# Another planned order for a two-part kernel, with five stores of 20 columns and three stores cut by rows

## The chip, the core and the metric

The kernel runs on one core of one Trainium2 chip. A core has a matrix engine (TensorE, PE in the profile), three other compute engines (VectorE = DVE, ScalarE = ACT, GpSimd = POOL) and SyncE (SP), each with its own in-order instruction stream, and sixteen DMA engines that move data between memory (HBM) and the core's on-chip memory. The metric is the device time of one execution in microseconds (us); the times given are medians of several runs.

## What is computed

```python
B, N, C = (4, 6400, 256)                       # q, k, v, float32
qn = q / (norm(q, axis=1) + 1e-06)             # the norm of each column over the 6400 rows
kn = k / (norm(k, axis=1) + 1e-06)
s = kn.transpose(0, 2, 1) @ qn / tau           # 256 x 256 for each of the 4 batches
a = softmax(s)
x = (v @ a).reshape(25600, 256)
# a mixture of 8 adapters of rank 16 on every row of x, the two best by x @ w_gate, softmax over the two
logits = x @ w_gate
for e in the two best:  x_out += w[e] * ((x @ A[e]) @ B[e])
```

All of q, k and v must have been read before the last row is written: 78.9 MB are read from HBM and 26.2 MB are written.

## The kernel before, in words

A batch has 6400 rows; partition p of the 128 holds rows 50p to 50p+49, called columns here, so a column is 128 rows of 256 numbers, 1 KB for each partition in float32. q and k are loaded in three pieces of 17, 17 and 16 columns (the names q10, q11, q12 stand for batch 1; a word such as q10 in the order loads the pair from q and k), v in five pieces of ten columns (v10 to v14). GpSimd issues all these loads (L578); they become bf16 on the way. Named steps, with the lines that issue them:

- G (L587 to L605): for each column, TensorE adds k'q to the accumulator (L593) and the squares that the norms need (L597 for k, L602 for q). For the groups of columns in OFF, the squares are left out here; ScalarE squares the group instead (sq, L615), VectorE adds the groups up (add, L621; red, L627) and TensorE sums over partitions at the end (n2p).
- After a batch's last column: norms, softmax and the product of a with the gate and A weights (n2, rsqrt, rq_ps, exp, aT, waA; L648 to L765), one short chain through three engines.
- For each piece of v: T transposes it (L788) and Te copies it out of PSUM; then either ZL (L812, gate logits and adapter inputs in one product, for the pieces in MERGED) or log (L826) and later Z (L879); a row of ten small gate steps on VectorE with one tanh on ScalarE; Ze (L890), gzT (L902), and Y (L915, L920), whose result Ye copies to the output tile y (L769 on ScalarE, L771 on VectorE).
- store (L928): SyncE issues the write of a piece of y, ten columns, 1280 KB. The last two pieces of the last batch go in parts of 4, 4 and 2 columns.

The order of all this comes from a planner in the file (Plan.run, L95): a list scheduler with a duration for each step and each engine, a rank from the place in WORDS (L402), and numbered buffers (STORE, L220: six banks of PSUM, six q/k tiles, three v tiles, four vT, seven y). It emits the steps in the order in which it started them, and each engine then executes its own in that order. HOLD (L409) names stores that must wait for a load: a tiny DMA that reads the last elements of the loaded tile (do_hold, L640, on SP ahead of the store) makes SP wait for the load's landing. OUT (L77) lets eight loads be on the way. SP's DMAs and ACT's use eight semaphores in turn; a DMA whose semaphore was last used by the DMA eight places before waits until that one has landed.

Of the kernel before, what the change touches and what calls it, by code (L numbers as in the profile page):

```python
# [18 lines left out]
class Step:  # L19
# [3 lines left out]
    def __init__(self, key, eng, deps, rank, take, give, size=0.0):  # L23
        self.packet = max(size, 0.08)
        self.key, self.eng, self.deps, self.rank = key, eng, deps, rank
        self.take, self.give, self.size = take, give, size
        self.users, self.place = [], {}
        self.ready, self.end, self.on = 0.0, None, None
        self.left = len(deps)
        self.only = next(iter(eng)) if len(eng) == 1 else None  # L30


class Clock:


    WINDOW, FIRST, LOW, HIGH = 3.413, 0.31, 0.5, 0.8
# [29 lines left out]
    SPARE = 1.0  # L66


class Plan:

    LAT = 0.07
    DMA_LAT = 1.8
    ENGINES = ("PE", "DVE", "ACT", "POOL", "SP")
    ISSUE = 0.55
    ISSUE_LAT = 1.8
    STORE_LAT = 1.4
    OUT = 8  # L77

# [15 lines left out]

    def run(self, head):  # L95
# [4 lines left out]
        loads, queue, stores = list(self.loads), [], []  # L100
        now, out, left = 0.0, 0, sum(s.key[0] != "warm" for s in self.steps.values())
        free["POOL"] = 0.2
        clock = Clock()

# [5 lines left out]
        def can_take(s):  # L110
            return all((kind, name) in held or self.store[kind] for kind, name in s.take)

        def start(s, eng):
            for kind, name in s.take:
                if (kind, name) not in held:
                    held[kind, name] = self.store[kind].pop(0)
                    s.place[kind] = held[kind, name]
            s.on = eng
            s.t = now
            self.out.append(s)  # L120

# [5 lines left out]
        while left:  # L127
            again = False
            if (loads and free["POOL"] <= now + 1e-9 and out < self.OUT and can_take(loads[0])):
                s = loads.pop(0)  # L130
                start(s, "POOL")
                out += 1
                free["POOL"] = now + self.ISSUE
                push(free["POOL"], "free", None)
                push(now + self.ISSUE_LAT, "asked", s)
                again = True
            for e in self.ENGINES:
# [3 lines left out]
                for s in wait[e]:  # L141
                    if not can_take(s) or (s.key[0] == "warm" and not clock.idle(now)):
                        continue
# [3 lines left out]
                    if best is None or (s.rank, s.seq) < (best.rank, best.seq):  # L147
                        best = s
# [9 lines left out]
                else:  # L158
                    push(free[e], "end", best)
# [3 lines left out]
            busy = [x for x in (queue, stores) if x]  # L163
            t = events[0][0] if events else float("inf")
            base = max(now, head)

            share = sum(x[0].packet for x in busy)
            if busy:
                t = min(t, base + min(x[0].size / x[0].packet for x in busy) * share)
            assert t < float("inf"), [s.key for s in self.steps.values() if s.end is None][:20]  # L170
            if t > base:
                for x in busy:
                    x[0].size -= (t - base) * x[0].packet / share
                    if x[0].size < 1e-6:
                        push(t + self.DMA_LAT, "landed", x[0])
                        out -= x is queue
                        x.pop(0)
            now = max(now, t)
            while events and events[0][0] <= now + 1e-9:
                _, _, what, s = heapq.heappop(events)  # L180
                if what == "asked":
                    queue.append(s)
                elif what == "store":
                    stores.append(s)
# [3 lines left out]
                elif what == "landed":  # L188
                    push(now + (SAFE if s.on == "POOL" else 0.0), "end", s)
                    for u in s.users:  # L190
                        if u.key[0] == "hold":
                            u.left -= 1
                            if u.left == 0:
                                push(now, "ready", u)
                elif what == "end":
# [6 lines left out]
                    for u in s.users:  # L202
                        u.left -= u.key[0] != "hold"
                        if u.left == 0 and u.eng and u.key[0] != "hold":
                            push(now + (0.0 if s.on == u.only else self.LAT), "ready", u)
# [5 lines left out]
NC = 50  # L211
# [4 lines left out]
V = ((0, 1), (1, 1), (2, 1), (3, 1), (4, 1))  # L216
# [13 lines left out]

def make_plan(B, order, ahead):
# [6 lines left out]
    for kind, b, i in order:  # L238
        if kind == "v":
            p.add(("load", "v", b, i, V[i][0] * PC, V[i][1] * PC), {}, (), 0, take=(("v", (b, i)),),  # L240
                  size=LOAD * V[i][1] * PC + 0.062)
            continue
        for c, n in PARTS.get((b, i), QK[i:i + 1]):
            for h in "qk":
                p.add(("load", h, b, i, c, n), {}, (), 0, take=(("qk", (h, b, i)),), size=LOAD * n + 0.062)

    for h in "qk":
        p.add(("cast", h), {"ACT": 0.6}, [("load", h, 0, 0) + PARTS[0, 0][0]], 0)
    p.loads[2].size += 0.5
    for b in range(B):  # L250

        for i, (c0, n) in enumerate(QK):
            for c in range(c0, c0 + n):
# [8 lines left out]
                p.add(("G", b, c), {"PE": 0.442 - 0.112 * sum((b, group_of(c), w) in OFF for w in "kq")}, deps,  # L262
# [4 lines left out]
        for w in "kq":  # L267
# [5 lines left out]
            for x, g in enumerate(halves):  # L273
                c, n = GROUPS[g]
                i = max(i for i, q in enumerate(QK) if q[0] <= c)
                p.add(("sq", w, b, g), {"ACT": 0.2 + 0.2125 * n},
                      [k for k in p.steps if k[:4] == ("load", w, b, i) and k[4] < c + n and c < k[4] + k[5]]
                      + [("cast", w)] * ((b, c) == (0, 0)), pos["qk", b, i] - SQ, take=(("ssq", (w, b)) if x == 0 else ("sq", (w, b, g)),),
                      give=(("qk", (w, b, i)),))
                if x:  # L280
                    p.add(("add", w, b, g), {"DVE": 0.15 + 0.268 * n},
# [4 lines left out]
            if halves:  # L286
                p.add(("red", w, b), {"DVE": 1.9}, [before], pos["qk", b, len(QK) - 1] - 1, give=(("ssq", (w, b)),))
                p.add(("n2p", w, b), {"PE": 0.35}, [("red", w, b), ("G", b, NC - 3)], -100, take=(("bank", ("n2p", w, b)),))
                late.append(w)
        if b == 0:  # L290
            p.add(("wts",), {"DVE": 1.8}, [("load", "k", 0, len(QK) - 1) + PARTS[0, len(QK) - 1][1]], -200)
# [3 lines left out]
        p.add(("accs", b, 1), {"ACT": 0.38}, [end], ch)  # L295
        p.add(("n2", b, 0), {"DVE": 0.45}, [end], ch)
        p.add(("accs", b, 0), {"ACT": 0.38}, [("n2", b, 0)], ch)
        p.add(("n2", b, 1), {"DVE": 0.45}, [("accs", b, 1)], ch)
        p.add(("rsqrt", b), {"DVE": 1.9 + 0.2 * len(late)},
              [("n2", b, 0), ("n2", b, 1)] + [("n2p", w, b) for w in late], ch, take=(("port", b),),  # L300
              give=(("port", b),) + tuple(("bank", ("n2p", w, b)) for w in late))
        p.add(("rq_ps", b), {"PE": 0.45}, [("rsqrt", b)], ch, take=(("bank", ("rq", b)),))
        for ic in range(2):
            p.add(("s", b, ic), {"DVE": 0.42}, [("rq_ps", b), ("accs", b, ic)], ch, give=(("bank", ("rq", b)),))
            p.add(("exp", b, ic), {"ACT": 0.68}, [("s", b, ic)], ch)
            p.add(("aT_ps", b, ic), {"PE": 0.14}, [("exp", b, ic)], ch, take=(("bank", ("aT", b)),))
        p.add(("recip", b), {"DVE": 0.17}, [("exp", b, 0), ("exp", b, 1)], ch)
        p.add(("aT", b), {"DVE": 0.42}, [("aT_ps", b, 0), ("aT_ps", b, 1)], ch, give=(("bank", ("aT", b)),))
        p.add(("waA_ps", b), {"PE": 0.35}, [("aT", b), ("wts",)], ch, take=(("bank", ("waA", b)),))
        p.add(("waA", b, 0), {"DVE": 0.35}, [("waA_ps", b), ("recip", b)], ch, give=(("bank", ("waA", b)),))  # L310
        p.add(("waA", b, 1), {"ACT": 0.38}, [("waA_ps", b), ("recip", b)], ch, give=(("bank", ("waA", b)),))
        p.add(("a", b), {"DVE": 0.5}, [("recip", b), ("aT", b)] + [("a", b - 1)] * (b > 0), ch + 1)

        for i in range(NP):
            v = max(g for g, (i0, _) in enumerate(V) if i0 <= i)
            x = pos["v", b, v] + 0.3 * (i - V[v][0])
            for u, (c, n) in enumerate(UNITS):
                p.add(("T", b, i, u), {"PE": 0.112 * n + 0.01}, [("load", "v", b, v, V[v][0] * PC, V[v][1] * PC)], x - ahead,
                      take=(("vT", (b, i)), ("bank", ("T", b, i, u))),
                      give=(("v", (b, v)),) if u == len(UNITS) - 1 else ())  # L320
                p.add(("Te", b, i, u), {"DVE": 0.16 + 0.125 * n, "ACT": 0.17 + 0.213 * n},
                      [("T", b, i, u)], x - ahead, give=(("bank", ("T", b, i, u)),))
            merged = (b, i) in MERGED
            if merged:
                for z, (c, n) in enumerate(ZUNITS):
                    p.add(("ZL", b, i, z), {"PE": 0.1145 * n + 0.005},
                          [("Te", b, i, u) for u, (c0, n0) in enumerate(UNITS) if c0 < c + n and c < c0 + n0]
                          + [("waA", b, ic) for ic in range(2)], x - ahead,
                          take=(("bank", ("ZL", b, i, z)), ("zl", (b, i))))
                    p.add(("ZLe", b, i, z), {"ACT": 0.17 + 0.1145 * n, "DVE": 0.14 + 0.142 * n},  # L330
                          [("ZL", b, i, z)], x - ahead, give=(("bank", ("ZL", b, i, z)),))
                prev = [("ZLe", b, i, z) for z in range(len(ZUNITS))]
            else:
                p.add(("log", b, i), {"PE": 0.55},
                      [("Te", b, i, u) for u in range(len(UNITS))] + [("waA", b, ic) for ic in range(2)], x - ahead,
                      take=(("bank", ("log", b, i)), ("gate", (b, i))))
                p.add(("loge", b, i), {"ACT": 0.27, "DVE": 0.27}, [("log", b, i)], x - ahead,
                      give=(("bank", ("log", b, i)),))
                prev = [("loge", b, i)]
            for name, eng, t in (("m1", "DVE", .27), ("eq1", "DVE", .27), ("lm", "DVE", .27),  # L340
                                 ("m2", "DVE", .27), ("msum", "DVE", .19), ("t", "DVE", .27),
# [645 lines left out]
```

## Time and profile before

| | |
|---|---|
| Median of 3 runs | 254.41 us (254.39 to 254.47) |
| The profiled execution | 254.46 us, its span (first to last instruction) 252.7 us: 1.8 us lie around it |
| Busy: PE, DVE, ACT, POOL | 217.8, 192.7, 151.1, 27.1 us |
| TensorE's granted clock | 0.986 of full |
| DMA packets | 11243, 66.70 MB |
| DMA queues, share of sixteen engines' span | loads 74.4%, stores and the first small loads 26.1%, ACT's first loads 0.8%, instructions 0.4% and 0.1% |
| Warm-up matmuls (L777), which only keep PE busy | 39 |

How to read it: the busy time of an engine says how much it did; what sets the end is told by the waits and by the chain that ended last. A DMA engine's share over 1.00 means that its packets overlap a little. For each DMA the trace also holds sixteen landing events, one for each DMA engine; they carry a time but not the engine's number, so the first and the last of the sixteen tell how far the engines are apart.

### The profile page before, as it was taken

The page shows a single profiled execution, that of the slowest core. Times are in us where ns is not written, and L with a number is a line of the kernel's source. Part 1 is how long each engine was busy: PE and PEld are TensorE (multiplying, and loading weights), DVE is VectorE, ACT ScalarE, POOL GpSimd, SP SyncE. Part 2 cuts the span into 40 slices and gives each one's busy share as a digit, 9 for nine tenths or more (in the row PEclk, how much of TensorE's full clock was granted, in tenths as well). Part 3 has the DMA queues.
Part 4 walks back from the last instruction along what each step waited for, and adds up shares of the span by engine and source line. Part 5 has one row for each costly group of instructions (what it writes and reads, how often), then busy time and mean ns, then how long its engine had stood idle before and what let it go on. Part 6 is the DMA issues. An engine that isn't in the chain of part 4 may idle for free.

```text
span 252.7 us, 5852 instructions
## 1 busy us (share of the span) xinstructions
PE 217.8 (86%) x2357; PEld 193.0 (76%) x2357; DVE 192.7 (76%) x528; ACT 151.1 (60%) x269; POOL 27.1 (11%) x54
## 2 busy tenths in 40 slices
PE   0274995988999998689999999889999979999990
PEld 0162882876999996579899899779999769999980
DVE  0055589869899987588899899489898898889850
ACT  5454427546786543975667768362674846657671
POOL 7003010040002002000500100500000000000000
PEclk9998899999999999999999999999999999999997
DMA  8999999999999999999999999999999999999996
GB/s 251 217 217 209 211 223 208 217 218 215 215 217 241 303 305 298 224 213 221 210 215 220 215 217 217 211 212 313 317 251 353 322 341 317 337 392 415 404 408 249
DMA packets 11243, 66.70 MB, mean 264 GB/s; under 512 B 1360, under 2 KB 1744, under 8 KB 6608
## 3 DMA queue, kind: packets, MB, share of 16 engines
q0 software_dynamic: 6912, 38.80, 74.4%
q1 hardware_dynamic: 3968, 26.87, 26.1%
q10 hardware_dynamic: 336, 0.66, 0.8%
q8 instruction: 18, 0.29, 0.4%
q14 instruction: 9, 0.07, 0.1%
HBM read 78.91 MB, written 26.21 MB: 416 GB/s over the span
## 4 chain that ended last, share of the span: by engine, by line
PE 53%; DMA 32%; issue 5%; DVE 4%; ACT 2%; POOL 1%; POOLq 0%; DVEq 0%
DMA v<-in_v_dram 18%; PE Y_ps L915 13%; PE acc L593 10%; DMA qk<-in_q_dram 10%; PE Y_ps L920 6%; PE T_ps L788 5%; PE ZL_ps L812 5%; DMA qk<-in_k_dram 5%; PE gzT_ps L902 4%; PE acc L597 3%; PE acc L602 2%; PE Z_ps L879 1%; ACT a_exp L715 1%; DVE a_bf L763 1%; PE log_ps L826 1%
## 5 line engine op out<-in xcount | busy, mean ns | idle before, releaser
L593 PE MATMUL acc<-qk 128*128 128x256 bf16 x400 | 69.6, 282 | 17.0 <-DMA qk<-in_k_dram 9.4
L915 PE MATMUL Y_ps<-a_bf,vT 128*128 128x256 bf16 x400 | 60.0, 273 | 0.2 <-DVE acc_sb L710 0.2
L621 DVE TENSOR_TENSOR ssq<-ssq,sq 128x1280 f32<-128x1280 f32 (+1 forms) x27 | 43.4, 1606 | 19.6 <-ACT sq L615 19.6
L769 ACT COPY y<-Y_ps 128x512 f32<-128x512 f32 x79 | 46.2, 586 | 16.6 <-PE Y_ps L920 13.5
L593 PEld LDWEIGHTS <-qk 128*128 128x128 bf16 x400 | 34.2, 101 | 20.7 <-DMA qk<-in_k_dram 11.5
L615 ACT ACTIVATE sq<-qk 128x1280 f32<-128x1280 bf16 (+1 forms) x27 | 36.9, 1368 | 17.7 <-DVE ssq L621 16.6
L915 PEld LDWEIGHTS <-vT 128*128 128x128 bf16 x400 | 38.9, 98 | 4.7 <-issue 0.3
L920 PE MATMUL Y_ps<-ball,gzT 128*128 128x256 bf16 x200 | 38.2, 273 | 0.0
L597 PE MATMUL acc<-qk 128*128 128x128 bf16 x242 | 34.5, 224 | 0.0
L788 PE MATMUL T_ps<-ident,v 128*128 128x128 f32 x200 | 27.6, 274 | 0.6 <-DVE waA_sb L757 0.4
L769 ACT COPY vT<-T_ps 128x512 f32<-128x512 f32 (+1 forms) x44 | 21.2, 510 | 10.9 <-PE T_ps L788 10.5
L597 PEld LDWEIGHTS <-qk 128*128 128x128 bf16 x242 | 24.4, 101 | 3.5
L890 DVE TENSOR_TENSOR gz<-zl,gateg 128x256 bf16<-128x256 f32 x70 | 26.3, 445 | 0.3
L578 POOL DMA_DIRECT2D v<-in_v_dram x20 | 11.5, 576 | 133.7 <-PE T_ps L788 92.8
L788 PEld LDWEIGHTS T_ps<-ident,v 128*128 128x128 f32 x200 | 22.3, 141 | 1.6 <-DVE waA_sb L757 0.6
L602 PE MATMUL acc<-qk 128*128 128x128 bf16 x168 | 23.4, 222 | 0.0
L902 PE MATMUL gzT_ps<-ident,gz 128*128 128x128 f32 x100 | 20.9, 281 | 2.6 <-DVE gateg L868 1.4
L920 PEld LDWEIGHTS <-gzT 128*128 128x128 bf16 x200 | 19.6, 98 | 2.3
L812 PE MATMUL ZL_ps<-waA_sb,vT 128*128 128x136 bf16 x280 | 19.5, 223 | 1.7 <-DVE waA_sb L757 1.5
L771 DVE COPY gzT<-gzT_ps 128x256 f32<-128x256 f32 (+1 forms) x40 | 15.0, 380 | 7.1 <-PE gzT_ps L902 5.6
L812 PEld LDWEIGHTS <-vT 128*128 128x128 bf16 x280 | 17.7, 98 | 2.4 <-issue 2.1
L615 ACT ACTIVATE ssq<-qk 128x1536 f32<-128x1536 bf16 x8 | 11.9, 1489 | 11.4 <-DMA qk<-in_q_dram 7.4
(80 smaller groups left out, 271.3 us busy)
## 6 DMA issues: line engine op xcount, KB each, us to landing
out_dram<-y SPq DMA_DIRECT2D x18, 1280.0 KB, 16.7
v<-in_v_dram POOLq DMA_DIRECT2D x20, 640.0 KB, 20.5
qk<-in_q_dram POOLq DMA_DIRECT2D x7, 1088.0 KB, 23.7
qk<-in_k_dram POOLq DMA_DIRECT2D x7, 1088.0 KB, 28.4
qk<-in_q_dram POOLq DMA_DIRECT2D x4, 512.0 KB, 19.2
qk<-in_k_dram POOLq DMA_DIRECT2D x4, 512.0 KB, 22.5
qk<-in_q_dram POOLq DMA_DIRECT2D x2, 1024.0 KB, 19.4
qk<-in_k_dram POOLq DMA_DIRECT2D x2, 1024.0 KB, 23.8
```

Source lines behind the costliest of these rows:

```text
L593: nc.tensor.matmul(acc[ic][:, 0:256], kt[:, j, ic::CC], qt[:, j, :], start=c == 0, stop=False, skip_group_check=True)
L597: nc.tensor.matmul(acc[ic][:, 256:384], kt[:, j, ic::CC], kt[:, j, ic::CC], start=False, stop=False, skip_group_check=True)
L602: nc.tensor.matmul(acc[ic][:, 384:512], qt[:, j, ic * P:(ic + 1) * P], qt[:, j, ic * P:(ic + 1) * P], start=False, stop=c == NC - 1, skip_ ...
L615: nc.scalar.activation(out[:, 0:n, :], t[:, j:j + n, :], ACT.Square)
L621: nc.vector.tensor_tensor(out=t, in0=t, in1=held["sq", (w, b, g), ""][:, 0:n, :], op=OP.add)
L769: nc.scalar.copy(out, in_)
L788: nc.tensor.matmul(ps[:, j, :], vt[:, c + j, :].bitcast(FP32), W["ident32"], is_transpose=True, start=(j == 0), stop=(j == n - 1))
L812: nc.tensor.matmul(ps[:, j, :], vT_of(b, i, c + j)[:, :, ic], st[b]["waA"][:, ic, :], start=(j == 0 and ic == 0), stop=(j == n - 1 and ic ...
L890: nc.vector.tensor_tensor(out=pairs[:, h].rearrange("p c (e r) -> p c e r", e=E), in0=z[:, 2 * h:2 * h + 2, :].rearrange("p c (e r) -> p c ...
L902: nc.tensor.matmul(ps[:, j, :], pairs[:, j * P:(j + 1) * P], W["ident32"], is_transpose=True, start=(j == 0), stop=(j == n // 2 - 1))
L915: nc.tensor.matmul(ps[:, j, :], vT_of(b, i, c + j)[:, :, ic], st[b]["a"][:, ic, :], start=(j == 0 and ic == 0), stop=False, skip_group_che ...
L920: nc.tensor.matmul(ps[:, j, :], pair[:, :, j], W["B"], start=False, stop=(j == 1), skip_group_check=True)
```

## The change

The diff does these things.

- The planner's durations, latencies and its picture of the DMA engines are other numbers and another code. Nothing of that is an instruction; it changes the order that the planner emits.
- WORDS: v00 is loaded ahead of q10, q11 ahead of v01, q20 ahead of v11, q22 ahead of v20. The rest of the sequence stays.
- OFF has 43 groups in place of 35 (241 columns in place of 195). MERGED has 10 pieces in place of 14. The planner emits 8 warm-up matmuls in place of 39.
- y is one tile of seven slots, v one of three. For five pairs of pieces ((0,0) with (0,1); (1,0) with (1,1); (2,0) with (2,1); (2,2) with (2,3); (3,0) with (3,1)) the planner takes two neighbouring slots and issues one store of 20 columns.
- The stores of (1,3), (2,4) and (3,3) go in four DMAs each, of 112, 6, 6 and 4 partitions; (3,3) is also still in parts of 4, 4 and 2 columns, so it becomes twelve DMAs.
- The three small DMAs of do_hold are gone; the store itself waits for the load. HOLD names other pairs.

SP's stores, in order, before: (0,2) (0,1) (0,3) (0,0) (1,0) (2,0) (0,4) (1,1) (1,2) (1,3) (1,4) (2,1) (2,2) (2,3) (2,4) (3,0) (3,1) (3,2) (3,3)x3 (3,4)x3. After: (0,3) (1,3)x4 (1,0)+(1,1) (1,4) (0,0)+(0,1) (2,0)+(2,1) (2,2)+(2,3) (0,4) (0,2) (1,2) (2,4)x4 (3,0)+(3,1) (3,2) (3,3)x12 (3,4)x3.

The core of the diff:

```diff
+PAIRS = {(0, 0), (1, 0), (2, 0), (2, 2), (3, 0)}
...
-WORDS = ('q10 v00 v01 v02 q11 v03 q12 v04 v10 v11 q20 v12 v13 v14 q21 v20 v21 v22 q22 q30 '
-         'q31 q32 v23 v24 v30 v31 v32 v33 v34')
+WORDS = ('v00 q10 q11 v01 v02 v03 q12 v04 v10 q20 v11 v12 v13 v14 q21 q22 v20 v21 v22 q30 q31 q32 v23 v24 v30 '
+         'v31 v32 v33 v34')
...
-HOLD = {(0, 0): ('k', 3, 1), (0, 1): ('k', 1, 2), (0, 4): ('k', 3, 2), (1, 0): ('k', 3, 1),
-        (1, 1): ('k', 3, 2), (1, 2): ('k', 3, 2), (1, 3): ('k', 3, 2), (1, 4): ('k', 3, 2),
-        (2, 0): ('k', 3, 1), (2, 1): ('k', 3, 2), (2, 4): ('k', 3, 1)}
+HOLD = {(0, 0): ('v', 2, 4), (0, 1): ('v', 0, 2), (0, 2): ('v', 3, 4), (0, 4): ('v', 3, 3), (1, 0): ('k', 3,
+        1), (1, 2): ('v', 3, 4), (2, 1): ('v', 1, 0), (2, 2): ('v', 1, 4), (2, 3): ('k', 2, 1), (2, 4):
+        ('v', 2, 1), (3, 0): ('k', 2, 0), (3, 1): ('k', 1, 0), (3, 4): ('v', 1, 1)}
...
+SPLIT, SHARES = {(1, 3), (2, 4), (3, 3)}, (112, 6, 6, 4)
...
-MERGED = {(0, 1), (0, 2), (0, 3), (1, 0), (1, 1), (1, 2), (1, 3), (1, 4), (2, 0), (2, 1), (2, 2),
-        (2, 4), (3, 2), (3, 4)}
+MERGED = {(0, 0), (0, 2), (0, 3), (0, 4), (1, 3), (2, 0), (2, 1), (2, 2), (3, 1), (3, 2)}
...
-    tiles = {}
+    Y = sbuf.tile([P, STORE["y"] * PC, C], FP32, name="y")
+    VS = sbuf.tile([P, STORE["v"] * PC, C], BF16, name="v")
...
     def do_store(s, b, i, c, n):
         lo = i * PC + c
-        nc.sync.dma_start(out_v[b, :, lo:lo + n, :], held["y", (b, i), ""][:, c:c + n, :])
...
+        at_y = at["y", (b, i)] * PC + c
+        p = 0
+        for rows in SHARES if (b, i) in SPLIT else (P,):
+            r = nc.sync.dma_start(out_v[b, p:p + rows, lo:lo + n, :], Y[p:p + rows, at_y:at_y + n, :])
+            if (b, i) in HOLD and not p:
+                tc.add_manual_dep(r.ins, loaded[held_by(plan, b, i)],
+                                  mybir.DependencyInfo(mybir.DependencyClass.Sync, mybir.DependencyReason.DATA),
+                                  reason="held")
+            p += rows
```

## The prediction, made before the changed kernel was run

> **What bounds the kernel now.** I read the page's DMA rows first. The second row of slices is the mean busy share of the sixteen DMA engines; the queue rows give each queue's packet time as a share of sixteen engines' span.
>
> ```profile
> DMA  8999999999999999999999999999999999999996
> q0 software_dynamic: 6912, 38.80, 74.4%
> q1 hardware_dynamic: 3968, 26.87, 26.1%
> q8 instruction: 18, 0.29, 0.4%
> ```
>
> Loads and stores together fill 100.5% of the span: no slice between the first and the last is under 90%. The table by stretches (busy us and instruction count of each engine, clock, DMA share, GB/s) shows what stands beside that late in the run.
>
> ```profile
> 115.00:180.00 65.00, 62.77 (x708) 57.64 (x707) 56.03 (x145) 39.79 (x72) 8.09 (x16) 1.00 1.04 231
> 180.00:235.00 55.00, 52.71 (x619) 48.28 (x618) 48.42 (x164) 35.53 (x81) 2.12 (x4) 1.00 1.03 341
> 235.00:246.00 11.00, 11.00 (x112) 9.93 (x110) 7.53 (x24) 7.89 (x16) 0.00 (x0) 1.00 0.96 400
> 246.00:250.00 4.00, 0.77 (x8) 0.44 (x5) 0.00 (x0) 1.25 (x3) 0.00 (x0) 0.90 0.97 386
> ```
>
> DMA is over 1.00 until 235; PE is busy to 96% from 115 on and to 100% from 235 to 246. Two things end close together. The last copy of y (ScalarE, 246.81 for 0.59 us) ends at 247.4, and its store is issued at 247.42. But the sixteen landing events of each store show that the engines do not end together:
>
> ```
> store, issued at        first engine landed   last engine landed
> (3,1)       233.23      238.73                242.68
> (3,2)       239.05      243.36                245.72
> last part   247.42      249.95                251.95
> ```
>
> The engine in front had nothing left between 238.73 and the store issued at 239.05; it is bound by the copies: its last parts landed 2.5 us after their issue. The engine behind never stopped: (3,2) came 3.04 us after (3,1), then the six parts (20 columns) took 6.23 us. The end is the work of the last DMA engine, 251.95, and 0.72 us after that the span ends. For (3,1) the sixteen stand at 0, 0.25, 0.35, 0.45; 0.79, 1.10; eight from 1.87 to 3.09; 3.81 and 3.95 us behind the first.
>
> **The change, part by part.**
>
> *Compute.* A column of G with both norms takes 0.44 us, with one 0.33: 0.11 for each norm. 46 columns more in OFF: -5.2 us on PE. A piece out of MERGED costs log 0.50 + Z 1.12 - ZL 1.18 = 0.44; four of them: +1.8. The 31 warm-ups that go (0.22 each) filled idle time. So PE has 3.4 us less. ScalarE gets eight squares (1.28 to 1.49), eight copies of y (0.59), sixteen of gzT (0.27 to 0.37), and loses eight of zl (0.40 to 0.50): about +17 on 151.1 busy of 252.7. VectorE gets eight adds and loses those copies:
>
> ```profile
> L621 DVE TENSOR_TENSOR ssq<-ssq,sq 128x1280 f32<-128x1280 f32 x15 | 22.3, 1487 | 5.8 <-ACT sq L615 5.7
> L621 DVE TENSOR_TENSOR ssq<-ssq,sq 128x1536 f32<-128x1536 f32 x12 | 21.1, 1754 | 13.9 <-ACT sq L615 13.9
> L771 DVE COPY y<-Y_ps 128x512 f32<-128x512 f32 x21 | 14.6, 701 | 4.1 <-PE Y_ps L920 4.1
> L771 DVE COPY gzT<-gzT_ps 128x256 f32<-128x256 f32 x28 | 11.8, 421 | 6.7 <-PE gzT_ps L902 5.2 <-ACT y L769 1.2
> ```
>
> 13 - 5.6 (8 x 0.70) - 6 (16 x 0.29 to 0.42) - 4 (8 x 0.43 to 0.58) = -3. I cost all this at nothing: the cover is the DMA work. Where the cover goes is rival D.
>
> *Order of the loads.* The bytes are the same, and every load still has its tile free in time, so the engines stay fed. v00 first puts k10 3.07 us later (one load of v, landings 49.88 to 52.97), and q11, k11 first put v01 some 10 us later: PE's emitted list has 25 us of work ahead of T of v01, which lands about 61.7 (k11 as computed, 58.6, and 3.07), so PE can have done 25 us then, where it had done 34 at 64 before. Nothing on the DMA side, below nothing on PE's; again rival D.
>
> *The three small DMAs go.* 48 packets of 2 B: nothing. SP has 0.5 us less three times, in front of stores that wait behind others: nothing.
>
> *Five double stores.* A store of ten columns takes an engine 3.04 us for eight rows, 0.38 a row (landings 235.69, 238.73); four columns take 1.24 / 8 = 0.156. So a column is 0.037 and a row's own cost 0.007; beside loads a 10 KB packet took 398 ns against 387 in the tail, 0.011 more. Five pairs save 5 x 8 = 40 rows on each engine: 0.28 us by the one, 0.72 by both; if a row of 20 columns is cut in two again, nothing. I take 0.5, between the two rows.
>
> *Three stores in parts.* 112 rows are seven for each of sixteen engines. The other 16 rows lie in parts of 6, 6 and 4, which can use at most 6, 6 and 4 engines. If all parts begin at the same engine, four engines get ten rows, two get nine and ten get seven. No row of the trace shows such a DMA. Bounds: the last engine loses one row of eight (-0.38 for ten columns), or gains two (+0.76), or nothing, if the rows are spread. In the offsets above four engines lead by over 3 us and two more by over 2.8 against the last: the pattern in which the shift would level them. I take -0.38 for each store, -0.76 by the time (3,3) starts.
>
> The Trainium skill, "DMA: Bandwidth & Descriptors", section "Why a DMA increments its semaphore by 16 and not by 1", says that a DMA issued from SyncE uses the largest number up to 16 that divides its rows, on the lowest-numbered engines; its section "Latency and other measured facts" says that engines 7 and 15 are usually slower than the rest. The trace has no engine numbers, but it has two stragglers (3.81 and 3.95, the next at 3.09). If they are those two, each split takes a row off both, -0.38; were they among the first four, +0.76.
>
> *The wait that this adds.* SP's DMAs use eight semaphores in turn, and the changed program makes each store wait for the store eight places before. Before, no store waited so: in SP's waits stores wait for copies, and DMAs appear only behind the end (L982) and before the small DMAs.
>
> ```profile
> SPq L928 <- DVE y L771: 111.6, 6, 73.0
> SPq L928 <- ACT y L769: 16.9, 9, 6.0
> SPq L982 <- DMA out_dram<-y: 3.8, 5, 1.2
> ```
>
> After, (3,3) is twelve DMAs. The first DMA of its third part (112 rows) waits until that of its first part has landed; the first part of (3,4) waits for the second part of (3,3), and for SP to have issued the four DMAs in between. SP's issues follow each other like this:
>
> ```profile
> 183.81 2.87 SPq L928 DMA_DIRECT2D out_dram<-y  x6
> ```
>
> 0.48 us each, 0.38 at the least. Behind them are queued the last ten columns, and nobody else but the end. On the path: (3,2) on the last engine 245.72 - 0.5 (pairs) - 0.76 (two splits) = 244.46. First part of (3,3), seven rows of four columns: 7 x 0.156 = 1.09, landed at 245.55. Four issues at 0.43 (between the two): 1.72, so (3,4) starts to be issued at 247.27, where it was issued at 245.45. From issue to landing on a free engine 1.21 us and the transfer (239.05 + 1.21 + 3.1 = 243.36), ten columns 1.24 + 1.24 + 0.64 = 3.12: 251.60. DMA runs dry in between: the third part holds 0.5 us of work, the gap is about 1 us, and it eats most of what pairs and splits bring.
>
> **Sum.** 251.60 against 251.95: -0.35 on the execution's own 254.46 gives 254.1; the median of the runs, 254.41, is as good as the same and gives 254.06. Forecast 254.1. By its bounds (issues 0.38 or 0.54, pairs 0.72 or 0.28) 253.7 to 254.8.
>
> **Rivals.**
>
> *B, the gain arrives.* The parts' issues are shorter than those of full stores, or SP's waits are met by then, and (3,4) is not held. Then the last engine has 0.5 + 3 x 0.38 = 1.64 less: 252.8. For it: no row shows an issue of six rows, and SP has nothing else to do. Against: the program's waits.
>
> *C, the rows land on the wrong engines.* The last engine is among the first six. Two splits then give +1.52 in place of -0.76, and the first part ten rows in place of seven, +0.47: 254.1 + 2.75 = 256.8; with nine rows, or rows spread evenly, 255.0 to 255.5. It decides as soon as one of the engines behind gains a row. Slower. Against: the pattern of the offsets.
>
> *D, compute becomes the bound.* The 9 us that PE is behind at 62 are not made up: PE has 3.4 less to do, so the last copy comes up to 5.6 later. It counts from the point where the last copy is later than 248.2 (the last issue in the sum above, 247.27 + 2 x 0.48), 0.8 us after today's: up to +4.8, 258.9; a third to a half of it 255.7 to 256.5. Place: Y (L915) and its copies in the last two pieces. Before, 165 us of listed work after 64 took the 183 us to 247, 9 of them idle; at that pace the 170 us after 62 end at 239.5 without a wait, and there is room for 8.7 us of waits, about as many as now. For it: there is no more room than that, and ScalarE has more to do. Against: in SP's order only one store goes ahead of the loads of q21, where three went between 77 and 90 (k21 landed at 126.5), so the loads of batches 2 and 3 come earlier by two stores, 6 us.
>
> **How the numbers follow.** 0.2% is 0.5 us, about what a measurement of this kernel can tell from no change: faster is under 253.9, slower over 254.9. The forecast's own case (A) 0.43, a third of it faster, the rest the same; B 0.25, faster; C 0.10, slower; D 0.22, slower. Faster 0.14 + 0.25 = 0.39, taken as 0.40; same 0.29, taken as 0.28; slower 0.32. Range 252.6 to 256.4: it takes in A, most of B, the smaller prices of C, and D up to nearly half its price.
>
> **What would show it.** Right: in SP's waits a store waiting for an earlier store, in the last 8 us; a dip of the DMA share there; the landings of the last store within 1 us of each other, where they are 2.00 apart; no idle DMA before 240. B: no such wait, last landing near 250.3. C: the last engine further behind than 3.95 after (2,4). D: PE's last Y after 248 and SP waiting for copies. I am wrong altogether if DMA has an idle stretch in the middle, where loads wait for tiles.

## The result, and the profile after

Forecast 254.1 us; the changed kernel takes 1.039 [1.037, 1.042] times as long as before, 264.4 us: **slower by 10 us**. The profiled execution below is a disturbed one of 268.5 us, whose second stop and DMA hole are larger than in the variants further down, so the sizes are read from those.

The DMA rows of the changed kernel's page answer to those shown of before: the slices, and the share of the queues.

```profile
DMA  8999999999999999999999998999996699999966
q0 software_dynamic: 6912, 38.80, 71.6%
q1 hardware_dynamic: 3232, 26.87, 25.5%
q8 instruction: 18, 0.29, 0.4%
```

Loads and stores fill 97.1% in place of 100.5%, with holes at 200 to 213 us and at the end. The table by stretches has the same columns as that of before:

```profile
115.00:148.00 33.00, 31.58 (x358) 28.64 (x357) 30.48 (x71) 24.83 (x41) 2.65 (x5) 1.00 1.03 219
148.00:165.00 17.00, 9.78 (x80) 8.32 (x78) 9.42 (x27) 7.54 (x9) 2.12 (x4) 0.80 0.96 224
165.00:185.00 20.00, 19.71 (x226) 17.57 (x224) 17.51 (x36) 12.32 (x23) 1.06 (x2) 1.00 1.00 255
185.00:198.00 13.00, 9.98 (x100) 8.82 (x98) 8.71 (x21) 5.77 (x12) 1.05 (x2) 1.00 1.03 301
198.00:205.00 7.00, 6.50 (x60) 6.04 (x60) 4.43 (x15) 3.66 (x9) 0.00 (x0) 0.52 0.88 270
205.00:222.00 17.00, 17.00 (x202) 15.69 (x201) 14.32 (x62) 14.76 (x37) 1.85 (x3) 1.00 0.78 226
245.00:258.00 13.00, 12.13 (x126) 10.72 (x123) 5.81 (x19) 9.30 (x18) 0.00 (x0) 1.00 0.87 333
258.00:266.70 8.70, 0.00 (x0) 0.00 (x0) 0.00 (x0) 0.00 (x0) 0.00 (x0) 0.58 0.66 237
```

PE has two stops, 148 to 165 and 185 to 205 us, each with its clock at half for a while (0.80 and 0.52 on average); the DMA hole at 205 to 222 comes after the second. And 8.7 us pass at the end in which only DMA works, at two thirds. The chain that ended last (start, us, what) names the cause of both stops:

```profile
143.22 0.35 SPq L972
143.62 0.38 SPq L972
144.04 0.28 SPq L972
144.36 14.11 DMA out_dram<-y
158.55 0.70 DVE y L813
159.29 1.01 PE n2p_ps L686 x4
...
184.03 0.70 DVE y L813
184.78 13.06 DMA out_dram<-y
197.86 0.59 ACT y L811
```

A copy of y waits until an earlier store has landed, because it writes into that store's slot. The planner put (1,2) into slot 3 behind (1,3): the other six slots were held by (0,0), (0,1), (0,2), (0,4) and the pair (1,0)+(1,1). It put the pair (2,0)+(2,1) into slots 5 and 6, of which 5 was behind (1,4): the other five were held by (0,0), (0,1), (0,2), (0,4) and (1,2). PE stands behind the copy: its next product needs a bank of PSUM that the copy has not emptied. The waits say the same (us in total, times, longest):

```profile
DVE y L813 <- DMA out_dram<-y: 10.4, 2, 6.8
ACT y L811 <- DMA out_dram<-y: 7.9, 3, 3.8
PE n2p_ps L686 <- DVE y L813: 6.9, 1, 6.9
```

And some rows of SP's own waits, with the same columns:

```profile
SPq L972 <- ACT y L811: 178.0, 7, 96.3
SPq L972 <- DVE y L813: 28.0, 3, 21.2
SPq L972 <- DMA qk<-in_k_dram: 18.4, 1, 18.4
SPq L972 <- DMA v<-in_v_dram: 11.2, 3, 7.3
SPq L972 <- DMA out_dram<-y: 0.4, 1, 0.4
```

The last row is the wait that the prediction put in the centre: 0.4 us. The two rows above it are the holds, where a store waits for a load. In the trace of before, no copy of y waits for a store. In e1, which has the new order and whole rows, the first stop is there too:

```profile
143.19 13.12 DMA out_dram<-y
156.31 0.03 issue
156.33 0.02 DVEq L813
156.35 0.04 issue
156.40 0.70 DVE y L813
```

**Where the 10 us are.** Last copy of y and end of the span in profiled executions (e1 to e5 are the variants below):

```
                                     last copy   span end   between
before                               247.4       252.7       5.3
whole rows (e1)                      250.7       256.3       5.6
whole rows for (3,3) alone (e2)      253.1       260.6       7.5
as changed, without holds (e3)       252.9       263.1      10.2
before with the three in parts (e5)  248.0       257.6       9.6
```

e3 took as long as the changed kernel (both 1.039 of before): 5.5 us are lost by the last copy and 4.9 behind it. With whole rows (e1) 3.3 and 0.3 of these are left. So about 7 us belong to the parts and about 3 to the order.

The order can be followed step by step: the planner in the file gives a time to each step, and the trace has one. The planner's own end is 251.8 us for the changed order and 252.3 for the one before, so it promised 0.5 us. PE's start of a step against the plan (median of the steps planned in 5 us from the time given; later is positive):

```
planned at       120    145    155    170    185    200    220    240
before           0.9   -0.0   -0.0    0.8    0.8    0.7    0.7    0.1
e1              -0.5   -0.5    5.8    4.2    3.5    4.1    4.4    4.4
e2              -0.4   -0.5    7.2    5.6    4.9    6.4    6.8    6.8
changed         -0.4   -0.4    7.1    5.3    4.6   11.0   11.4   11.4
```

The planned last copy ends at 246.4; with the lateness of 240 that is 250.8 for e1, 253.2 for e2, 257.8 for the changed kernel, which each trace has within 0.1 us. Of what is late at 155 us, 2.3 to 2.5 us are made up by 185; the second wait then adds 0.6 us in e1 and 1.5 in e2 (6.4 in the changed kernel's execution), and from 200 us on nothing is made up.

### The profile page after: what moved, and what is told of

It is laid out like the page before. It is cut to its first block, busy times and chain, and to the rows that moved or that the text cites. A ratio compares the mean times of both kernels' runs of the same rounds, so it can differ in the third digit from the quotient of the medians.

```text
span 266.7 us, 5745 instructions
## 1 busy us (share of the span) xinstructions
PE 219.2 (82%) x2314; PEld 193.7 (73%) x2314; DVE 187.2 (70%) x504; ACT 168.2 (63%) x297; POOL 27.3 (10%) x54
## 4 chain that ended last, share of the span: by engine, by line
PE 50%; DMA 28%; DVE 10%; ACT 6%; issue 2%; POOL 1%; SPq 0%; ACTq 0%; DVEq 0%; POOLq 0%
DMA qk<-in_k_dram 18%; PE Y_ps L956 15%; DMA out_dram<-y 10%; PE Y_ps L961 7%; PE T_ps L829 6%; PE acc L643 5%; PE gzT_ps L943 4%; DVE ssq L671 4%; ACT sq L665 4%; PE Z_ps L920 3%; PE ZL_ps L853 3%; PE log_ps L867 2%; PE acc L647 2%; PE n2p_ps L686 2%; DVE gz L931 2%
## 5 line engine op out<-in xcount | busy, mean ns | idle before, releaser
L671 DVE TENSOR_TENSOR ssq<-ssq,sq 128x1536 f32<-128x1536 f32 (+1 forms) x35 | 56.9, 1625 | 24.5 <-ACT sq L665 24.5
L665 ACT ACTIVATE sq<-qk 128x1536 f32<-128x1536 bf16 (+1 forms) x35 | 48.3, 1381 | 26.1 <-DVE ssq L671 17.9
L811 ACT COPY y<-Y_ps 128x512 f32<-128x512 f32 x87 | 50.4, 588 | 22.3 <-PE Y_ps L961 11.5
L643 PEld LDWEIGHTS <-qk 128*128 128x128 bf16 x400 | 38.2, 107 | 24.7 <-DMA qk<-in_k_dram 14.3
L956 PEld LDWEIGHTS <-vT 128*128 128x128 bf16 x400 | 39.3, 100 | 4.8 <-issue 0.4
L829 PE MATMUL T_ps<-ident,v 128*128 128x128 f32 x200 | 30.1, 282 | 5.6 <-DMA v<-in_v_dram 5.2
L647 PE MATMUL acc<-qk 128*128 128x128 bf16 x166 | 23.1, 220 | 0.0
L652 PE MATMUL acc<-qk 128*128 128x128 bf16 x152 | 21.9, 228 | 0.0
L931 DVE TENSOR_TENSOR gz<-Z_ps,gateg 128x256 bf16<-128x256 f32 x50 | 19.2, 443 | 0.4
L931 DVE TENSOR_TENSOR gz<-zl,gateg 128x256 bf16<-128x256 f32 x50 | 18.7, 446 | 0.2
L647 PEld LDWEIGHTS <-qk 128*128 128x128 bf16 x166 | 16.3, 98 | 2.0
L813 DVE COPY y<-Y_ps 128x512 f32<-128x512 f32 x13 | 8.5, 686 | 12.8 <-DMA out_dram<-y 10.4
L652 PEld LDWEIGHTS <-qk 128*128 128x128 bf16 x152 | 14.9, 103 | 2.1
```

The source lines that it names most:

```text
L643: nc.tensor.matmul(acc[ic][:, 0:256], kt[:, j, ic::CC], qt[:, j, :], start=c == 0, stop=False, skip_group_check=True)
L647: nc.tensor.matmul(acc[ic][:, 256:384], kt[:, j, ic::CC], kt[:, j, ic::CC], start=False, stop=False, skip_group_check=True)
L652: nc.tensor.matmul(acc[ic][:, 384:512], qt[:, j, ic * P:(ic + 1) * P], qt[:, j, ic * P:(ic + 1) * P], start=False, stop=c == NC - 1, skip_ ...
L665: nc.scalar.activation(out[:, 0:n, :], t[:, j:j + n, :], ACT.Square)
L671: nc.vector.tensor_tensor(out=t, in0=t, in1=held["sq", (w, b, g), ""][:, 0:n, :], op=OP.add)
L811: nc.scalar.copy(out, in_)
```

## The experiments

**e1, e2: rows whole, or whole for (3,3) alone.**

```diff
-SPLIT, SHARES = {(1, 3), (2, 4), (3, 3)}, (112, 6, 6, 4)
+SPLIT, SHARES = set(), (112, 6, 6, 4)              # e1
+SPLIT, SHARES = {(1, 3), (2, 4)}, (112, 6, 6, 4)   # e2
```

> The changed kernel with every store of whole 128 rows (no parts of 112, 6, 6 and 4); same planned order, same holds. Theory 1 (output slots: five of the seven y slots are held by late stores, so the copies of the next pieces wait for the few stores that circulate): the store of (1,3) still lands 12 us after its issue beside loads, and (2,0) still waits for the store of (1,4); only the tail's issues and 2 to 3 us at (1,3) go: 257 to 260, from 264.4. Theory 2 (the parts: 15.3 us from issue to landing at (1,3), and 10 us of issues in the tail): most of the loss goes with them, 254 to 256.

> The changed kernel with (3,3) stored without parts of rows; (1,3) and (2,4) still in parts. Both theories: the time from the last copy of y to the last landing, 8.2 us in the changed kernel's profile and 4.5 before, falls to about 4.5: 260 to 261. Theory 2 has the rest of the loss in the parts of (1,3), theory 1 in the slots; this run prices the tail alone.

e1: 1.012 [1.009, 1.016], 257.4 us, by the first theory; e2: 1.032 [1.026, 1.037], 262.4, more than expected, because 6.6 us still pass from the last copy to the last landing in place of about 4.5. In e1 the copies of (1,2) come at 156.3 (157.9 in e2, with parts), those of (2,0) at 193.6 (195.9).

**e3, e4: no store waits for a load**, with parts and with whole rows. The plan, its slots and the order of SP's stores stay.

```diff
-            if (b, i) in HOLD and not p:
+            if False:
```

> The changed kernel with no store waiting for a load (the planned order on every engine is unchanged, the parts stay). Theory 1: the store of (1,0) with (1,1) is issued near 145 in place of 163 and (0,0) with (0,1) long before 192, so slots come free earlier and the stall of 13 us at (2,0) goes; the one at (1,3) stays: 255 to 260. Theory 2: the stall at (1,3) and the tail are the parts', which stay: 262 or more. Against both: stores that go early delay the loads behind them, and the time is no better.

> Both at once: no store waits for a load and all stores are of whole rows. Theory 1: 252 to 256, clearly less than with whole rows alone. Theory 2: the same as with whole rows alone, within 1 us.

e3: 1.039 [1.036, 1.041]; e4: 1.017 [1.012, 1.021]. Nothing gained. SP no longer waits 18.4 us for k31, but the slots were dealt out by the planner, and (1,2) still waits for (1,3), (2,0) for (1,4). The theory that the holds cost the time falls.

**e5, e6: the parts in the kernel before**, all three or (1,3) and (2,4) alone.

```diff
-        nc.sync.dma_start(out_v[b, :, lo:lo + n, :], held["y", (b, i), ""][:, c:c + n, :])
+        p = 0
+        for rows in (112, 6, 6, 4) if (b, i) in SPLIT else (P,):
+            nc.sync.dma_start(out_v[b, p:p + rows, lo:lo + n, :], held["y", (b, i), ""][p:p + rows, c:c + n, :])
+            p += rows
```

> The kernel before, its order and its stores of 10 columns unchanged; alone the stores of (1,3), (2,4) and (3,3) go in parts of 112, 6, 6 and 4 rows. Theory (the parts cost time by themselves where the store's landing or SP's next issue is waited for, which here is the case in the tail alone): 257 to 259 us, the last copy where it was (247 to 248 us), and 2.5 to 4 us more from the last copy to the end, with issues of over 1 us on SP after 241 us. Rival (the parts level the DMA engines, as the prediction counted them, and cost only beside the new order): 253.5 to 254.5 us.

> The kernel before; alone the stores of (1,3) and (2,4) go in parts of 112, 6, 6 and 4 rows, the last ones stay whole. Theory (nothing computes or loads late because of these two landings in this order): 254 to 255.5 us. Rival A (parts level the engines): 253.5 us or less. Rival B (a part beside loads holds a DMA ring by about 1.7 us wherever it stands): 257 us or more.

e5: 1.019 [1.018, 1.021], +4.9 us; e6: 1.008 [1.005, 1.011], +2.0. Both are a little more than their theories had. The last copy is nearly where it was (248.0 and 247.4, before 247.4). SP's last issues, from the timeline of before and of e5 (start, us, count):

```profile
241.10 6.65 SPq L928 DMA_DIRECT2D out_dram<-y  x6
```

```profile
241.72 12.14 SPq L931 DMA_DIRECT2D out_dram<-y  x15
```

The twelve DMAs of (3,3) in e5, in groups of 112, 6, 6 and 4 rows, start of issue and us:

```
4 columns   241.72 0.33   242.10 1.22   243.37 2.31   245.73 0.68
4 columns   246.51 0.32   246.88 0.34   247.26 1.25   248.72 0.58
2 columns   249.92 0.32   250.37 0.27   250.98 0.27   251.30 0.29
(3,4)       252.21 0.36   252.66 0.38   253.13 0.73
```

(3,4) is ready at 248.0 and goes out at 252.2. The waits for semaphores are the ones that the prediction derived: the issue at 249.92 follows the landing of the first part's 112 rows (249.85), that at 252.21 the landing of the second part's (252.15). The twelve issues take 8.2 us together, but the four between these two waits take 1.67, where the forecast had 1.72; the long ones lie ahead. What is late is the landings, and they are late already at (3,2): its last engine lands at 248.70, in before at 245.72.

The landings of (2,4) show one reason. In e6, where its four DMAs have sixteen, six, six and four landing events, the last of each come at 238.26, 238.64, 239.42 and 239.84; the next behind the last in the 112 rows came at 236.06, and the other three of the four rows by 234.78. So the engine that is last also carries a row of each small part: ten rows, where a whole store gives it eight. e5 has the same: 235.67, 236.02, 236.79, 237.22 at (2,4), and 249.85, 250.35, 250.97, 251.15 at the first part of (3,3). After (2,4) this engine of e6 lands its rows 6.2 to 6.9 us behind the first (4.0 in before), in the last store 5.6 us behind, 3.3 behind the last but one. That is rival C, in the order before.

The other reason is in the single rows. A row of ten columns takes 0.39 us as a rule. After 225 us each of the five kernels with parts (changed, e2, e3, e5, e6) has 6 to 13 rows that took over 0.8 us, up to 2.39; the eleven without parts have at most one each, the longest 1.36 us. Of the rows of four columns (0.16 us), 46 took over 0.3 us in e5 and 2 in before. While (3,2) lands in e5, two rows took 1.19 and 1.82 us, 2.2 us above the usual, and its last engine lost 2.3; that these were its rows is not shown, since a row's record does not name the engine. Nor is it shown what slows the rows.

**e7: another slot for (1,2) and (1,4).** Whole rows; (0,4) loses its hold, its store moves to where it is computed, and the slots are set by hand.

```diff
+    early_y = [x for x in steps if x.key[:3] == ("store", 0, 4)]
+    steps.remove(early_y[0])
+    steps.insert(1 + max(n for n, x in enumerate(steps) if x.key[:3] == ("Ye", 0, 4)), early_y[0])
     at = {(kind, name): n for s in steps for kind, name, n in s.got}
+    at["y", (1, 2)], at["y", (1, 4)] = 4, 3
```

> The changed kernel with whole rows, and one store moved: (0,4) is stored as soon as it is computed (about 107 us) instead of held for (3,3)'s load, and its slot 4 goes to (1,2); slot 3 goes to (1,4), so that neither (1,2) waits for the store of (1,3) nor (2,0) for that of (1,4). Instruction order on all engines but SP is unchanged. Theory (the two waits for y slots are what is left of the loss when rows are whole): copies of (1,2) start by about 150 us instead of 156.3, those of (2,0) by about 188 instead of 193.6, 252.5 to 255 us in all. Rival A (the loss is in the order of the loads, or in warm-ups left out): 257 to 258.5 us as with whole rows alone, with PE waiting for loads in place of y slots. Rival B (the store that now goes early delays the loads as much as the slots did): the copies of (1,2) on time, but G of batch 2 later by 5 us, 257 us or more.

1.013 [1.010, 1.016]. It was less clean than I wrote: without the hold the planner itself planned anew, and the other engines' order changed too. No copy waits more than 0.6 us for a store any more ((1,2) at 134.3, (2,0) at 184.9), and PE is at no time after 60 us later than its plan by more than 1 us (medians as above); but this plan ends at 255.3, and so does the span, at 255.4. The store that goes early takes its place from loads: k21 lands at 123.0 in place of 120.5. That the loads lose in this way all that the slots gain is the planner's account; the chip kept to it.

**e8, e11: (1,3) stored by columns as they are ready**, in whole rows; in e11 also the last two columns of (1,2) in spare room. Order, slots and holds are unchanged. The lines are e11's; e8 does the same to (1,3).

```diff
+    n = next(n for n, x in enumerate(steps) if x.key == ("store", 1, 3, 0, PC))
+    steps[n] = Step(("store", 1, 3, 8, 2), {}, [], 0, (), ())
+    for c in (4, 0):
+        n = max(n for n, x in enumerate(steps) if x.key[:3] == ("Ye", 1, 3) and x.key[3] < c + 4)
+        steps.insert(n + 1, Step(("store", 1, 3, c, 4), {}, [], 0, (), ()))
```

> The changed kernel with whole rows; the store of (1,3) goes in three stores of 4, 4 and 2 columns, each as soon as its columns are copied (about 134.3, 140.2 and 143.3 us), so that the slot of (1,3) comes free by columns. Every instruction keeps its place on every engine; slots, holds and loads are the same. Theory (with whole rows, what is left of the loss begins where the copies of (1,2) wait for the landing of (1,3)'s store, 3.3 us later than the plan has it, and PE, stopped behind them, falls to half clock): copies of (1,2) from 150 us or before instead of 156.3, no half clock from 157 to 164, T of (2,0) near 163 to 165 instead of 168, last copy near 247 instead of 250.7, 253.5 to 255.5 us. Rival (this wait is made up later anyway, and the loss is in the second wait, of (2,0) for the store of (1,4), or in the end): copies of (1,2) earlier, but copies of (2,0) still at 193 to 194 and 257 to 258 us.

> The changed kernel with whole rows and its instruction order on PE, DVE and ACT unchanged, holds and loads too. (1,3) is stored in columns (4 at about 134.2, 4 at 140.2, 2 at 143.3 us), and the last 2 columns of (1,2) are copied to 2 spare columns instead of slot 3 (the room comes from three tiles of the gate that share their place with three others), so that no copy of (1,2) waits for a store issued after 141 us. Theory (with whole rows the chip keeps the plan's times until the copies of (1,2) wait for (1,3)'s store, which lands 3.6 us later than planned; the order is fixed, so that every later step is late by as much): copies of (1,2) done by 154 to 155 us, PE no more than 1.5 us behind the plan between 155 and 185 us (it was 5.8 to 3.7), and, if (1,4)'s store lands within 1.5 us of the plan, the last copy at 246.5 to 248.5 and 254 to 256 us in all. If the store of (1,4) lands late as well, PE is behind by that much from 190 us on, and no more. Rival (the lateness comes back by other ways, such as loads or half clock): PE behind by 3 us or more between 160 and 185 us with (1,2)'s copies in time, 257 us or more.

e8: 1.013 [1.011, 1.015]. Its last two columns, issued at 143.2, landed at 157.7, so that the copies of (1,2) began at 151.6 but ended at 158.4. e11: 1.011 [1.009, 1.014]. PE against the plan in e11: 2.8 us at 155, 1.3 at 170, 0.6 at 185, then 2.4 at 190, when (1,4)'s store lands at 192.0 (planned 189.4), and 2.8 to the end; last copy 249.1. Shortening the first wait shortened the lateness up to 185 as the theory has it; the second wait then gave half of it back. In time the two differ from e1 by less than their intervals: e8 came out as its rival had it, and e11 missed its 254 to 256 us. So the waits are shown as the place where PE falls behind; that removing one brings back time is not.

**e9: the pairs in two stores of ten columns.**

```diff
+            wide, n = n, min(n, PC)
             r = nc.sync.dma_start(out_v[b, p:p + rows, lo:lo + n, :], Y[p:p + rows, at_y:at_y + n, :])
+            if wide > n:
+                nc.sync.dma_start(out_v[b, :, lo + n:lo + wide, :], Y[:, at_y + n:at_y + wide, :])
```

> The changed kernel with whole rows; each of the five pairs still waits until both pieces are computed and for its one held load, but goes in two stores of 10 columns, one right behind the other. It prices the wide rows alone. Prediction's term: pairs give about 0.5 us, so 0.3 to 0.8 us slower than with whole rows alone (257.5 us by its fast runs). Rival (a row of 20 columns took 804 ns in the trace and one of 10 columns 400 ns, so wide rows give nothing by themselves): within 0.5 us of it either way. Rival B (halves bring the first half's slot free sooner, (1,4) and (2,0) move up): faster by 1 us or more.

1.013 [1.011, 1.015] against 1.012 [1.009, 1.016] for e1: wide rows are worth nothing that this can tell. The two intervals leave about 1 us open, twice the prediction's term.

**e10, e12: other orders from the same planner**, whole rows, picked from many settings by the planned times that the expectations tell. Only the planner's constants differ (here e12's second one; AHEAD, SQ, HOLD, OFF and MERGED too).

```diff
-PAIRS = {(0, 0), (1, 0), (2, 0), (2, 2), (3, 0)}
+PAIRS = {(0, 0), (1, 0), (2, 3), (3, 1)}
...
-WORDS = ('v00 q10 q11 v01 v02 v03 q12 v04 v10 q20 v11 v12 v13 v14 q21 q22 v20 v21 v22 q30 q31 q32 v23 v24 v30 '
-         'v31 v32 v33 v34')
+WORDS = 'v00 q10 q11 v03 v02 v01 q12 v04 v10 q20 v11 v12 v13 v14 q21 q22 v20 v22 v21 q30 q31 q32 v23 v24 v32 v31 v30 v34 v33'
```

> Whole rows, and another order out of the changed kernel's own planner: load order, holds, pairs, halves and merged pieces were chosen so that the planned time stays low when every store before 200 us lands 0, 1.5, 3 or 4.5 us later than the planner has it: 252.0, 251.9, 253.3 and 254.3 us, against 251.8, 257.3, 255.6 and 259.7 us for the changed order. Theory (the changed order's 251.8 holds only where each store lands on the planner's instant; on the chip (1,3) and (1,4) land 3 to 4.5 us later): the kernel before stood 2.1 us above its plan, so 254 to 256.5 us, with the copies that wait for a slot no more than some 2 us behind the plan at 200 us. Rival (what is left of the loss is not the landings but the common features of the new order: few warm-ups, 7 slots with pairs, one load order up to q22): 257 to 258.5 us again.

> As the other one, from another start of the choice: planned 253.8 us with no delay and 251.9, 253.5 and 254.9 with 1.5, 3 and 4.5 us. Theory: 254.5 to 257 us. Rival: 257 to 258.5 us.

> Whole rows, the changed kernel's planner, 7 slots and five pairs; load order, holds, pairs, halves and merged pieces chosen by another test than in the two orders before: each order is planned once and then replayed unchanged on every engine while stores land later (1.5 us all, or 3.6 us those of 130 to 160 us, or those of 160 to 205 us, or loads 0.3 and stores 0.5). This order's end stays at 251.8 us in the first four and 252.3 in the last; the changed order's goes from 251.8 as planned to 256.7 with (1,3) 3.6 us late, its last copy to 250.9 (with whole rows the chip had 250.7). Theory (a fixed order hands a late landing on to the end): the kernel before stood 2.1 us above its plan, so 253.6 to 255.5 us, last copy by 247. Rival (few warm-ups, pairs and the new load order cost 3 us whatever the landings do): 257 to 258.5 us, with PE 3 us or more behind the plan before the first copy that waits for a store.

> As the other one, another order: planned 251.9, and replayed with (1,3) landing 3.6 us late 254.1 us, last copy at 248.3 in place of 245.1; with all stores 1.5 us late 251.9. Theory: as (1,3) is stored at 144.6 beside loads here too, 254 to 256.5 us, slower than the other one by 0.5 to 2.5. Rival: 257 to 258.5 us.

e10: 1.016 [1.013, 1.019] and 1.028 [1.023, 1.034]; e12: 1.014 [1.011, 1.017] and 1.008 [1.006, 1.009], 256.3 us, the fastest of the new orders. Missed: e10 both, e12's first. e10 was chosen wrongly: I let the planner plan again under each delay, but the chip has one order. e12 missed in another way. Its first order kept to the plan from 60 to 210 us (steps at most 2.8 us early and 1.5 late), so that neither pairs nor few warm-ups cost anything before that; then PE waited for a load:

```profile
215.17 0.28 PE L930 MATMUL gzT_ps<-ident,gz 128*128 128x128 f32 x1
215.28 1.04 PE L816 MATMUL T_ps<-ident,v 128*128 128x128 f32 x8
216.16 0.60 PE L943 MATMUL Y_ps<-a_bf,vT 128*128 128x256 bf16 x4
216.59 0.38 PE L948 MATMUL Y_ps<-ball,gzT 128*128 128x256 bf16 x2
216.81 0.38 PE L816 MATMUL T_ps<-ident,v 128*128 128x128 f32 x2
222.20 1.08 PE L816 MATMUL T_ps<-ident,v 128*128 128x128 f32 x4 [5.01 <-DMA v<-in_v_dram]
```

That load of v landed on the first DMA engine at 215.6 and on the last at 222.1: 6.5 us apart, where the planner reckons with about 2.3 (SPREAD and SKEW, 0.6 and 0.008 for each us). PE was 7.7 us late from there on and 8.2 at the end. The second order was 4.5 us late at 155, where (1,3)'s store had its engines 5.4 us apart, and 4.8 at the end.

So a landing is that of the last DMA engine, the planner has one spread for all of them, and a fixed order keeps most of what it loses. In e1 the planner gives each load up to 147 us within 0.5 us of its last landing (one at 2.0), and the stores' flights within 1.5 us, but for one: (1,3), 13.1 us in place of 9.5, its sixteen landings 4.3 us apart. A replay of that order by the planner's own rules, nothing moved and (1,3) 3.6 us late, has the last copy at 250.9; the chip had 250.7. Not settled is why the engines lie 4 to 5 us apart just then. Five kernels (e1, e4, e9, e10's and e12's second) store (1,3) at 143 to 144 us with one load, k30, still to be moved, and had 4.2 to 5.4 us; stores between 140 and 157 us with two or three loads on the way had 1.4 to 2.0 (e7, e12's first), but 4.3 in e10's first. In the five the gap is there before the store lands: q30's landings are 2.4 to 2.8 us apart, those of k30 behind it 3.9 to 4.3. That the engines in front run ahead with the store where they have no load row to alternate with is only argued. No version tried beats the kernel before.

## Why the prediction was wrong

- **"Every load still has its tile free in time, so the engines stay fed"** is the step that failed for the order. It speaks of the tiles of loads and never of the slots of y, through which a late store stops a copy, a bank, PE, and then the loads. In e1, without parts, this costs 3.3 us at the last copy. The sign that the prediction named for being wrong altogether, idle DMA with loads waiting for tiles, is there as well, at 180 to 185 us. The DMA share is the last number but one, first of before, then of e1 (0.80 in e2); the load of v issued at 181.93 in e1 had waited 7.3 us for PE's T.

```profile
180.00:185.00 5.00, 5.00 (x53) 4.54 (x52) 4.20 (x15) 4.06 (x8) 0.00 (x0) 1.00 1.05 267
180.00:185.00 5.00, 5.00 (x60) 4.72 (x60) 4.50 (x12) 3.84 (x9) 0.53 (x1) 1.00 0.74 127
```

- **Parts, -0.38 a store**, is the other step that failed, and the larger one: the three together cost 4.9 us in the order before, 6.9 in the new one. The sum had (3,2) landed on the last engine 0.76 us earlier by two splits; in e5 it landed 3.0 us later. Levelling did not happen: the last engine got a row of each small part, rival C's mark, and rows beside the parts took longer than any price in the sum. Beside loads each small part also prolonged (1,3)'s flight: the 112 rows landed by 155.4, the parts of 6, 6 and 4 rows by 155.7, 157.4 and 158.5. The Trainium skill, "DMA: Bandwidth & Descriptors", section "Why a DMA increments its semaphore by 16 and not by 1", from which the prediction drew which engines gain rows, agrees with the trace in how many engines a part uses (six, six and four landing events); their numbers are not in the trace. If they are the lowest ones, the last engine is not one of the two that the prediction took from the page.
- **The added wait**: the mechanism was right (the two gaps in e5), and so was the price of an issue where it counts, 1.67 us for four against 1.72. The landings that are waited for were late, by the parts. From the last copy to the end the forecast had 4.9 us (251.60 and 0.72, less 247.4), before had 5.3, and e5 has 9.6.
- **Rival D** (the last copy late, 0.22) came true by its sign and place: 250.7 in e1 to 253.1 in e2. Its cause was another: at 120 us PE was 0.4 us ahead of a plan that ends 0.5 us before the old one, and it lost the time in two waits.
- **Pairs, -0.5**: not seen; e9 differs from e1 by 0.001 in ratio, known to about 0.004. A row of 20 columns took 804 ns in the changed trace, one of 10 columns 400; in e1 783 and 391. So the row's own cost that the term was built on does not show.
- **Compute at nothing**: held in the sense that PE, VectorE and ScalarE were never the bound before 143 us. **The three small DMAs at nothing**: held for them; the holds that took their place cost nothing either (e3).
- **The range** ended at 256.4: waits for slots had no chance in it, and the parts no price above two rows of a DMA engine.

## What to carry to other kernels

Where an order is fixed ahead, follow every buffer whose next user waits for a DMA's landing, stores first, and ask what that landing is worth if its last engine is 4 us late: here the order absorbed little of it. A planner's gain of 0.5 us in 250 is smaller than one such landing, and says nothing about the chip. Before cutting a DMA into parts, read one such part in a trace: which engines land its rows, and how long the rows beside it take.

## What the runs showed of the hardware

- A DMA of six rows took SP 0.27 to 2.31 us to issue at the end of e5, the ones of 112 rows beside it 0.32 or 0.33. A whole store can take long too (1.15 and 1.37 us once each in e1). What the issue waits for is not in the trace.
- Beside DMAs of six and four rows, single rows of 10 KB took up to 2.39 us (e2), where 0.39 is usual.
- The sixteen landings of one store lay between 0.2 and 8.0 us apart (the last stores of e5, and (1,0)+(1,1) in e3), and the gap grew from 2.5 to 4.0 us from one load to the next (q30 and k30 in e1).
- After PE's stop at 150 us the granted clock was at half for 3.4 us in e11 (158.1 to 161.5), 6.8 in e1 (157.1 to 163.9) and 10.3 in e2 (154.9 to 165.2), so that a wait cost more than its length at first: in e1 (1,3) landed 3.3 us after its planned time, and PE was 5.8 late at 155.
